# Unscaled softmax rows, 1/sum through DRAM, and masks by GpSimd in an attention and feed-forward kernel

## The chip, the cores and the metric

One core of one Trainium2 chip. Its engines are TensorE (PE in the profile; its weight loads are PEld), VectorE (DVE), ScalarE (ACT), GpSimd (POOL) and SyncE (SP, which here issues nearly all DMAs). The metric is device time in microseconds for one execution.

## The reference

Batch 8, 8 heads, 576 rows, head size 64; then a feed-forward block on 4608 rows of 512 with a hidden size of 768.

```python
scores = q @ k.T / sqrt(64)                    # for each batch and head
thresh = max(scores, -1) - tau                 # tau = 0.02
scores = where(scores >= thresh, scores, -1e9)
attn = exp(scores - max(scores, -1))
attn = attn / (sum(attn, -1) + 1e-9)
x = (attn @ v), heads side by side             # 4608 x 512
h = maximum(maximum(x @ w1, x @ w2), x @ w3)
out = h @ w_out
```

So each row of the softmax keeps only the scores within tau of its maximum, and each row is divided by its own sum.

## The kernel before

**Tiles.** Four heads of one batch make a quad (16 quads, `g`). Its 4 x 576 rows are 18 half tiles of 128 rows by 576 scores: nine chunks `c` of two halves `r` (the two pairs of heads). In all there are 144 chunks, 288 halves. Chunk 4 of a quad holds the ninth 64 rows of two heads together, so that its partitions 0 to 63 and 64 to 127 belong to different heads. Two quads make a batch's 512 columns of x, on which the feed-forward block runs: six hidden tiles of 128 for each of three weights (`hid` in `ffn`), then the output chunks (`outp`, and `ninth` for the odd 64 rows). The last batch is cut into two parts of rows (`SPLIT`).

**The path of a half.** `scores` puts 128 x 576 into PSUM (TensorE). `maximum` (DVE) copies it to a tile `z` in SBUF, negated, and takes the row's maximum in the same instruction (`accum_out`). Then one of four ways, set by a digit for each half in `MASKED`:

- 0: `threshold` (DVE, one column), Prelu (ACT) that flattens all above the threshold's distance, Exp with the row sum (ACT). Two passes on ACT.
- 1: Exp (ACT), then a compare-and-multiply with the row sum (DVE, `scalar_tensor_tensor`). One pass on each.
- 2 and 3: as 0 and 1, with ACT reading the scores from PSUM (`direct`) and not from `z`.

All of these write into `z` in float32. When both halves of a chunk have their sums (`sm`, two columns), `reciprocals` takes 1/sum (DVE), and `normalized` multiplies each half by it on GpSimd, into the bf16 tile `P` of 128 x 1152. `turned` issues a DMA transpose of `P` from SP into `ptq`; with it `product` multiplies by v into PSUM as x transposed (64 columns of x by 576 rows, two heads on 128 partitions). x is evacuated to `xt` in bf16, one half of the products by DVE (`on_vector`), the other by ACT (`on_scalar`).

**Buffers.** `z` has 9 tiles, and from the 72nd half on two more are borrowed from the pool `stage`, whose other use is loading the weights in the first part (`half_of_z`). `P` has 6 tiles. PSUM is four slots of 128 x 1024, shared by everything that TensorE writes.

**The order.** `_Ordered` ties the instructions of each engine to the order in which the program names them. That order is written out by hand as a text, `ORDER`: each letter issues one step (with a digit for the PSUM slot where it starts one), and `issue` gives the letters their meaning. S: scores of a half; m: `maximum`; s: `threshold`; e: `exponents`; n: the second ACT pass; k: the DVE mask; r: `reciprocals`; p: a scaling pass on GpSimd; t: `turned`; T: transposes of q and k, evacuated by a (ACT) and c (DVE), with copies q on GpSimd; O: a product, evacuated by x (ACT) or w (DVE); F and B: the two halves of a feed-forward group, evacuated by h (ACT), v (DVE) and u (ACT); l: loads; o and i: stores; g and z: loading and casting of the weights; y: casts of v. So an engine does the steps that fall to it in the order of the letters, and waits where one is not ready. The line number of nearly all instructions in the profile is that of the helper in `_Ordered` (L93).

Of the kernel before, what the change touches and what calls it, by code (L numbers as in the profile page):

```python
# [15 lines left out]
OP = AluOpType  # L16
# [5 lines left out]
FLAT = 2.0 ** -100  # L22

MASKED = """
232222322322222222021032222202332122123122200200111000000000100000000011
000010111020011000101000000001100001001000010011111100000000100100000000
110010030111000100010000000001010100001110001011010100110000000000000000
100101101011000000120000001010000000110011100000001110001000010011111021
# [6 lines left out]
MORE_Z = 72  # L35
# [5 lines left out]
llllllglllT0laclT1laclzllqqS0qqS1meS2mS3lmlT0enlkS1ylmlT2eamelrnpS3leqlmnyS1qcapS0emtnrcS3pmnT2qmepgrelS1qya  # L41
gS0pmelT2mqnS3tcpemqS2nlkT1eytaS0rmnT1kpermS3yS2enczrmS1qT0enmepnqtS3nprmaymgpeS0lptS2mppT0mtpS1enencnqsS3re
rmtpS0mS1penmS3lqnsS2mtperpekzllmT0tmpenkT1pgS3eearnS0petmnqrS2meqlnpS3lmnplsS2cetpremS1pS0nmplermtzeS3mnS2p
mtnpmS3rkpS1leektS0emnrpmemptS1eekS2pO3mktS0rennmpermT2pnS1wptemS3prkyO0tmeakS2pgS1enxlnrmS0lpesS2mezT3mS1np
mgntspcS2eqrseT3mtpeS0srmapS1mnT2ptS3mnqO0ceqmeO1prswnptnkS3pxS0meF1meS2zBresmT0qghF3klpF2nkBtaS1sveS0pemF3B
nyrrsmyBepT1svS0hpcT2nS3zmaS1erpgsF2mntpsBmnS3yvF1etssT0myeBprS2cnpS3mnS0ympelF2epF3lmBnzslssvS0htBrqmeS2vpn
S1gF0sepmF3teqBmF2erssvpBtnBkphF0eS1vtS3znmF2nrBmqteS1rpvBnS3pmlnF0pmgeS1qsBsrhmS3pevS2npS1mF0npsO3ermpesmO2
zewepgsskBxtT3nF1vS2nklBarS0mlphS3mtepF2sS1rmnyBmetF3pvT0eBpcnS2tzT1nvS0asmzS3temS2qeS1meF0trkpmS3lenpBmnlys
reklpF1umerpskS3upBeoketmS0uS2umpS3tesmS1qeT0myO2nqlrsnlprcO3etqsmepwS0xptS1mnF3psnmS2BlerskpS1thF0meF3pmeBF
2ktnBveBsrS1nvpS0hmyF3emF2npBrssT0eprtvBaF1kS3nqvBeF0myhyS2kyleF3mBelBvnpS2snsS0vptemS1pnF3rmpT2tnBmpeF0scS1  # L50
htBrnmpF3erT2rpvlBasS1pstvnS2pmeF0pS3emtBqnmT2S1hcqS3empF2eS0rsqmtS1epsmBeF3pmnF0stsvBeBknF2klhF1BvelS0nrvpB
emT3pS2arvS0ptnS3mpnO1smtesrkpeF2swnlrpmeT0S1qtescS3epBmnpmnT0trskS3paS1umS0ulqmeS3lmyS1nopS2smelS0rmeS3psmn
O1ypersmqO2etkpemO0lewqxlknpS3tS1keF2momS3lexF0ktT1enkBercpnsBpumN1ertkphkF3jS0rursS1empBnmF2ptS0vpS1smeF3yt
BsnsmBpnvS0pT1hmF2atT3srepS0cF1eprBsmeqF3vnByBynvplS2nsS0plmhS1mteS2mF0nF3mteS1rrspBnmS2pelvBlepF1smT0leqBvl
aS2rkhF3oqnsS0mtS1epmBeqsF2ssmtS0epvBeyF1mnF3vpBesrS0ktphBermS1npT2svO0nytmpncT3eS1wF2nrmS0aBrsmnqF3vnT1pS0c
eBptsF2mhpS1eS3pmteS0qmBeO1spmnkteF3rvnpT0BsskapS2xvS0erS1qmtnS3pmnF2mqlespmeS1rtkBepresmT3puS1cuS0ptmnS3pS2
meyS1lrekpF0tnsmempO3lekteskO2nrsmpeBkpxrnwS1uptS3muS2pnmF0yoeS1mF3lesymBtnS2srkpS1hmBeF0spveF2ertBmpT3nrsvS
1paBlmpnS0tS3qhmF1epsmS2leBymF3tevF0nBknlS1rsvpS2esmqnBF3srmhpS1epS0tmeF2pssBrempBtesvS0ynF1mT3lnpBvF0lhsrcS
2tnT1mBnF3valS2nrBsqmeF0pvS1epS2meBptsmS3eqF1hmT2peBcS3tnskT2O0arkplnmO2lerpvewptS3xkpS1nF2meF0sstreBsmpS3nv
pBnmS1tS2hmT3eF0rmpnF1cBpnBrevptT3S2apvS0qmtS3S1enmqF2esrsqmiepmleS0soykeS1plBnmemtS3ukS0uT1snrlO2cpekynO1me  # L60
ymeF3pwxskteS0keS1BrrnkopmF2pmS0BqeuurtsmF1phS3srnpS2meT0ptBmeS3ykpaN2esvempF0tS1jkpF3ermBeS2ptvnS1pmBnS0rls
hsmpS2elF3mqntS1mpF0nsrBskpeF2lsmBetBpveF1yhvS3lnkS2lesF0mytnBmBerqsS3veF2lpvnF1pBsmT0htBceF3rT2vnpBsaS0pvnF
1qmtS2nBsrnmT0pS3hrcpF2esS1mpteS0rmpS3emBpntF1svqnS0ssBmpeoT2vO3lamtneF1wS0nrlBpmeS3qsrS2hsmS0pnmF1eptS3smeB
pmF2ntS0veS3rsmnpS1BnpO0veytrempS2empS3xsmS1tekF0nsknlT2rmpBelmlpnscS3quS1umyS2eorT0kpeO3tmeyO1ewlepsmF3etka
rknS2qklT0nBmxespcS2eryF0mpF1uskpuBtnS2BhmqF3nsvS0peS2srmtpF1eBmpeF0srvnBptS2hyS3pmeF1lmeBlBevtF3nkT2S0arrvp
BnS2mphS1smpF0ntS3smnpBmeF1lsT2esvlF3nrBrcptBnvpS2eS0qmlhS1tsnprsmT3F2epmS0aptBemF3yevS1oS0nqmBnpsrS2mnF1ptv
S0epmBeS3mthS2skeF0F1snmlBeklO3ersvpnrmByepF0swT2eqtBvnqF3ssrcS1hpiBmpT0S2vaptS1snmS0pnT3mqF2tecT1BarmS3pnS1
vqeS0mF2pesrmnptmS3npT1seS0qctBeymqermpS1eS3mpuF0nmtuskS1eS2klnS3smBesrsepO1upmemO2txrkpukeO3wnkpS0xS2emF3et
rmS1pnBssspmF2hS0rtepS3mnBpmF1etS0veF3mnN2rnpBpjF0evtF2esBkBkhF1nsvS3eBmBevO3hrkS2pwnS1mnF3prmS2eptsF0mnBpsS
1sevyS2terBmpeF3svS1iyepBmoS0yhmtF2ekF3nBsmS1ersBvpnF0pmeF2BvteS1hBmF3rsS0vpeF1rknpBBmnO2vhptO0xrpnS3pwS2trm  # L70
npS0mnF3pmteF1pBeBvtS0rS2vpS3empF1ktkF0kBereskpemBkperumO2uptO3xpN1wtenkO2jrF3pxF1hpF2nvF3tvF1rhF2pvF3pvF1hF
2tvF3vF1hF2voF3vF1ohF2vF3vF1hF2vO3vO1wF2xuuF1oF0hiF3vF1vF0hF3vF1vF0hF3vF1vF0hF3vF1vF0hF3vF1vF0huF3vF1ovF3uoF
0uoN1fjdi
# [31 lines left out]
def kernel(  # L105
# [44 lines left out]
    def weight_loads():  # L150


        def piece(dst, src):
            my = {}

            def load():
                my["t"] = stage.tile([128, 4 * 256], F32, name="stage")
# [19 lines left out]
    small = ctx.enter_context(tc.tile_pool(name="small", bufs=6))  # L177
# [177 lines left out]
    halves_of_z = iter(range(1 << 20))  # L355

    def half_of_z():

        n = next(halves_of_z)
        if n >= MORE_Z and (n - MORE_Z) % (ZBUFS + 2) >= ZBUFS:  # L360
            return stage.tile([128, 4 * 256], F32, name="stage")[:, :S]
        return zz.tile([128, S], F32, name="z")

    def maximum(c, r):

        z = c["z", r] = half_of_z()
# [8 lines left out]
    def threshold(c, r):  # L375
        th = c["th", r] = small.tile([128, 1], F32, name="th", bufs=5)
        vector.tensor_scalar(out=th, in0=c["nm", r], scalar1=-1.0, scalar2=tau, op0=OP.mult, op1=OP.subtract)
# [22 lines left out]
    def normalized(c):  # L400
        c["P"] = P = pp.tile([128, W], BF16, name="P")
        for n in range(2):
            pool.tensor_scalar(out=P[:, n * S:(n + 1) * S], in0=c["z", n],
                                    scalar1=c["rs"][:, n:n + 1], scalar2=1.0, op0=OP.mult, op1=OP.mult)
            if n:
                line["t"].append(c)
            yield
# [7 lines left out]
    def product(L, r, target, part=None):  # L415
# [26 lines left out]
        def on_vector():  # L442
            ps = st["ps"]
            dst = target(L["b"])[:, 2 * L["qd"] + r, :]
            vector.tensor_copy(out=dst[:, lo:hi], in_=ps[:, base:base + hi - lo])

        def on_scalar():
            ps = st["ps"]
            dst = target(L["b"])[:, 2 * L["qd"] + r, :]
            scalar.activation(out=dst[:, lo:hi], in_=ps[:, base:base + hi - lo], func=AF.Copy)  # L450
        p = _Piece((L["b"], L["qd"], r, part), first)
        p.vector = on_vector if r == 0 else None
        p.scalar = on_scalar if r == 1 else None
# [25 lines left out]
    def ffn(b, part):  # L479
# [87 lines left out]
        def ninths_of_two():  # L567
# [11 lines left out]
            def done():  # L579
                ob = hp_.tile([128, DM], F32, name="ob9", bufs=1)  # L580
# [12 lines left out]
        def ninth():  # L593
# [10 lines left out]
            def done():  # L604
                ob = hp_.tile([128, DM], F32, name="ob9", bufs=1)[:, 0:DM // 2]
# [36 lines left out]
    Ls, xts, stores, stores9, ends, ninths = {}, {}, [], [], [], []  # L642
# [20 lines left out]
    vector.memset(vrs[2], 0.0)  # L663
    for t in vrs[0:2]:
# [33 lines left out]

    def flow(what, fn):
        while True:  # L700
            yield from fn(line[what].pop(0))
# [5 lines left out]
                O=products(), F=pieces(), N=iter(lambda: ninths.pop(0), None))  # L707
    line = {k: [] for k in "menkrptahvuxwcqsjf"}
    casts = iter([w[1] for w in wl])
    loads = iter([w[0] for w in wl])  # L710
    flows = dict(p=flow("p", normalized), q=flow("q", lambda x: swapped(*x)),
# [7 lines left out]
    def issue(what, where):  # L719
# [10 lines left out]
        elif what == "O":  # L730
            p = next(todo["O"])
            p.first(where)
            for k, fn in (("x", p.scalar), ("w", p.vector)):
                if fn:
                    line[k].append(fn)
# [11 lines left out]
        elif what == "m":  # L747
            c, r = line["m"].pop(0)
            maximum(c, r)
            line["e"].append((c, r))  # L750
            if not masked(c["g"], c["idx"], r) and not direct(c, r):
                line["s"].append((c, r))
        elif what == "s":
            threshold(*line["s"].pop(0))
# [4 lines left out]
        elif what in "nk":  # L759
            c, r = line[what].pop(0)  # L760
# [69 lines left out]
```

## Time and profile before

| | |
|---|---|
| time of three runs | 446.69, 446.92 and 449.09 us; median 446.92 |
| profiled execution | span of 444.8 us from its first to its last instruction; a time of its own beside that is not listed, and the median of the runs lies 2.1 us above the span |
| busy | PE 422.4, DVE 392.8, ACT 403.0, POOL 311.9 us |
| mean granted TensorE clock | 0.988 |
| DMA | 88.5 MB, 213,959 packets |

The page gives the busy time of an engine as the union of its instructions, and a string of 40 digits, tenths of busy time in 40 equal slices of the span. In a group's row stand the engine, the operation, out<-in with the names of the tiles, the shapes, the count, then busy us, mean ns of one, and the idle time before them with what ended it. `z<-sc` is written from the scores in PSUM; `stage` in place of `z` is a borrowed buffer.

### The profile page before, as it was taken

The numbers are of one execution on the slowest core, as the hardware profiler recorded it, in microseconds if no ns is written. First come the engines' busy times: TensorE is split into PE (matmuls) and PEld (weight loads), VectorE is DVE, ScalarE is ACT, GpSimd is POOL, SyncE is SP. The second block draws the span as 40 slices with busy tenths as digits, with TensorE's granted clock in tenths as the row PEclk, the third lists the DMA queues.
The fourth block names the chain that finished last, engine by engine and source line by source line (L and its number), as shares of the span: only waits on it lengthen the run. The fifth ranks groups of instructions, "written<-read, shape, count | busy, mean of one in ns | idle before, by whom it ended". The sixth has DMA issues, their size and how long they took to land.

```text
span 444.8 us, 14254 instructions
## 1 busy us (share of the span) xinstructions
PE 422.4 (95%) x5188; PEld 320.2 (72%) x5190; DVE 392.8 (88%) x1228; ACT 403.0 (91%) x836; POOL 311.9 (70%) x420
## 2 busy tenths in 40 slices
PE   7767789999999999999999999999999999999996
PEld 6334347787788767787788777788688886787873
DVE  3887999999999999999999999998999998899642
ACT  3999999999999999999999999899999999987632
POOL 2799989997878687696785877676676685457400
PEclk8998999999999999999999999999999999999999
DMA  7999999999999999699899999989999977487633
GB/s 188 275 293 199 291 169 269 235 243 262 229 180 194 212 222 292 125 256 167 143 234 189 230 198 203 209 168 210 208 206 194 244 151 105 83 179 136 145 116 108
DMA packets 213959, 88.50 MB, mean 199 GB/s; under 512 B 189184, under 2 KB 202240, under 8 KB 213888
## 3 DMA queue, kind: packets, MB, share of 16 engines
q1 hardware_dynamic: 213360, 86.96, 95.9%
q8 instruction: 41, 0.67, 0.6%
q10 hardware_dynamic: 528, 0.62, 0.5%
q14 instruction: 30, 0.25, 0.2%
HBM read 35.65 MB, written 9.44 MB: 101 GB/s over the span
## 4 chain that ended last, share of the span: by engine, by line
PE 86%; ACT 5%; DVE 4%; issue 2%; DMA 1%; SPq 0%; DVEq 0%; ACTq 0%
PE ph L93 32%; PE sc L93 32%; PE po L93 10%; PE o L93 9%; ACT z L93 5%; PE tp L93 3%; DVE z L93 3%; DMA qm<-in_q_dram 1%; ACT qt L93 1%; SPq L93 0%; DVE xt L93 0%; DVE hm L93 0%; DVE stage L93 0%; DVE rs L93 0%; ACT ob L93 0%
## 5 line engine op out<-in xcount | busy, mean ns | idle before, releaser
L93 POOL TENSOR_SCALAR P<-z,rs 128x576 bf16<-128x576 f32 x250 | 200.6, 814 | 63.3 <-DVE rs L93 28.1
L93 DVE TENSOR_SCALAR_CACHE_REDUCE z<-sc 128x576 f32<-128x576 f32 x250 | 183.7, 750 | 14.8 <-PE sc L93 10.1
L93 PE MATMUL sc<-kt,qs 64*128 64x256 f32 (+2 forms) x640 | 182.6, 423 | 5.7 <-DVE z L93 2.3
L93 PE MATMUL sc<-kt,qt 64*128 64x320 f32 (+2 forms) x640 | 182.4, 433 | 5.2 <-ACT z L93 3.3
L93 PE MATMUL ph<-xt,w 64*128 64x288 bf16 (+2 forms) x2160 | 170.8, 283 | 0.1
L93 PEld LDWEIGHTS <-w 64*128 64x128 bf16 (+1 forms) x2160 | 130.1, 94 | 28.6 <-issue 4.3
L93 ACT ACTIVATE z<-z 128x576 f32<-128x576 f32 x174 | 117.6, 679 | 0.1
L93 PEld LDWEIGHTS sc<-kt,qs 64*128 64x128 f32 (+1 forms) x640 | 92.4, 180 | 25.7 <-DVE z L93 5.7
L93 ACT ACTIVATE z<-z,th 128x576 f32<-128x576 f32 x143 | 106.2, 769 | 5.0 <-DVE th L93 4.2
L93 PEld LDWEIGHTS sc<-kt,qt 64*128 64x128 f32 (+1 forms) x640 | 91.9, 179 | 19.7 <-ACT z L93 5.9
L93 DVE SCALAR_TENSOR_TENSOR z<-z 128x576 f32<-128x576 f32 x76 | 62.2, 830 | 0.5 <-ACT z L93 0.5
L93 PE MATMUL po<-wo,hT 64*128 64x512 bf16 (+3 forms) x454 | 53.5, 354 | 0.3
L93 POOL COPY qs<-qt 64x640 f32<-64x640 f32 (+3 forms) x66 | 43.0, 652 | 10.8 <-ACT qt L93 7.2
L93 ACT ACTIVATE z<-z,nm 128x576 f32<-128x576 f32 x68 | 50.6, 767 | 0.0
L93 DVE TENSOR_TENSOR hm<-ph,hm 128x576 bf16<-128x576 f32 (+2 forms) x54 | 37.0, 686 | 9.2 <-PE ph L93 8.9
L93 ACT ACTIVATE hm<-ph 128x576 bf16<-128x576 f32 (+2 forms) x54 | 31.8, 589 | 13.4 <-PE ph L93 12.8
L93 POOL TENSOR_SCALAR P<-stage,rs 128x576 bf16<-128x576 f32 x38 | 30.4, 804 | 19.3 <-ACT z L93 5.4
L93 PEld LDWEIGHTS <-hT 64*128 64x128 bf16 (+2 forms) x456 | 30.0, 95 | 16.5 <-issue 2.3
L93 DVE TENSOR_TENSOR hT<-ph,hm 128x576 bf16<-128x576 f32 (+2 forms) x54 | 37.0, 686 | 4.0 <-PE ph L93 2.3
L93 PE MATMUL o<-ptq,vb 128*64 128x64 bf16 (+2 forms) x544 | 39.0, 281 | 0.0
L93 ACT ACTIVATION_READ_ACCUMULATOR z<-z 128x1 f32 x174 | 34.3, 197 | 0.0
L93 PEld LDWEIGHTS <-vb 128*64 128x64 bf16 x544 | 23.3, 111 | 12.8 <-issue 4.9
(45 smaller groups left out, 431.6 us busy)
## 6 DMA issues: line engine op xcount, KB each, us to landing
vm<-in_v_dram SPq DMA_DIRECT2D x32, 256.0 KB, 4.8
qm<-in_q_dram SPq DMA_DIRECT2D x15, 512.0 KB, 5.0
km<-in_k_dram SPq DMA_DIRECT2D x15, 512.0 KB, 5.3
out_dram<-ob SPq DMA_DIRECT2D x14, 512.0 KB, 4.0
stage<-in_moe_w_dram SPq DMA_DIRECT2D x9, 512.0 KB, 5.2
ptq<-P SPq DMA_TRANSPOSE x144, 4.0
vr<-in_v_dram SPq DMA_DIRECT2D x16, 128.0 KB, 3.4
stage<-in_moe_w_out_dram SPq DMA_DIRECT2D x3, 512.0 KB, 4.9
```

Of the source, the lines that this page charges most:

```text
L93: ins = fn(*a, **kw)
```

## The change

- `P` is written directly by the last step of a half, in bf16 and unscaled (ACT's Exp or DVE's mask). `normalized`, its letter p and the scaling pass are gone.
- The sums of a quad (or of a quad's part, in the last batch; 18 units) stand in one tile `sm` of 20 columns. `reciprocals` works once for a unit: one reciprocal of the columns and one that moves the odd 64 rows to the partitions of their own place (three in the last batch's second part, one in its first), then a 32 x 32 block transpose of 128 x 32 on DVE. The letter D stores the result to a tile `rows` in DRAM (32 x 128), and R loads it back twice, broadcast over 64 partitions each, into a tile of `stage`, 128 x 2 x 576.
- All evacuations of x are on DVE now, as a product of PSUM and that tile (letter w); x of the letters is gone.
- A fifth digit, 4, stands at 13 halves, ten of them among the first 72: `threshold` takes the negated maximum plus tau, `set_apart` (letter b) makes three passes on GpSimd: subtract the threshold and multiply by 2 to the 100th (into `P`, bf16), maximum with 0, add to `z`. Then one Exp with the row sum on ACT (letter X). The digits 2 become fewer, 1 more.
- `z` borrows no buffers of `stage`; the two tiles of `stage` are 1152 wide; `ob9` uses a `z`. `small` has 8 buffers.
- `ORDER` and `MASKED` are new as a whole.

```diff
+FAR = 2.0 ** 100
...
-        if n >= MORE_Z and (n - MORE_Z) % (ZBUFS + 2) >= ZBUFS:
-            return stage.tile([128, 4 * 256], F32, name="stage")[:, :S]
-        return zz.tile([128, S], F32, name="z")
+    def by_pool(c, r):
+        return by_mask[2 * number[c["g"], c["idx"]] + r] == "4"
...
+        if by_pool(c, r):
+            vector.tensor_scalar(out=th, in0=c["nm", r], scalar1=tau, scalar2=None, op0=OP.add)
...
+    def half_of_p(c, r):
+        if "P" not in c:
+            c["P"] = pp.tile([128, W], BF16, name="P")
+        return c["P"][:, r * S:(r + 1) * S]
...
+    def set_apart(c, r):
+        z, m = c["z", r], half_of_p(c, r)
+        pool.tensor_scalar(out=m, in0=z, scalar1=c["th", r], scalar2=FAR, op0=OP.subtract, op1=OP.mult)
+        pool.tensor_scalar(out=m, in0=m, scalar1=0.0, scalar2=None, op0=OP.max)
+        pool.tensor_tensor(out=z, in0=z, in1=m, op=OP.add)
...
     def numerators(c, r):
-        z, acc = c["z", r], c["sm"][:, r:r + 1]
-        if masked(c["g"], c["idx"], r):
-            vector.scalar_tensor_tensor(out=z, in0=z, scalar=thr, in1=z,
+        z, p, acc = c["z", r], half_of_p(c, r), sum_of(c, r)
+        if by_pool(c, r):
+            scalar.activation(out=p, in_=z, func=AF.Exp, bias=c["nm", r], scale=-1.0, accum_out=acc)
+        elif masked(c["g"], c["idx"], r):
+            vector.scalar_tensor_tensor(out=p, in0=z, scalar=thr, in1=z,
                                         op0=OP.is_ge, op1=OP.mult, accum_out=acc)
         else:
-            scalar.activation(out=z, in_=z, func=AF.Exp, scale=-1.0 / FLAT, accum_out=acc)
-    def reciprocals(c):
-        c["rs"] = small.tile([128, 2], F32, name="rs")
-        vector.reciprocal(c["rs"], c["sm"])
-    def normalized(c):
-        c["P"] = P = pp.tile([128, W], BF16, name="P")
-        for n in range(2):
-            pool.tensor_scalar(out=P[:, n * S:(n + 1) * S], in0=c["z", n],
-                                    scalar1=c["rs"][:, n:n + 1], scalar2=1.0, op0=OP.mult, op1=OP.mult)
...
+            scalar.activation(out=p, in_=z, func=AF.Exp, scale=-1.0 / FLAT, accum_out=acc)
...
+    def reciprocals(g, part, n):
+        L, t = Ls[g], turns[n % 2]
...
+            vector.reciprocal(new[:, :, f:f + 9], sums[:, :, f:f + 9])
...
+            vector.reciprocal(new[to, :, at:at + 1], sums[of, :, was:was + 1])
+        vector.transpose(t[:, 1, :], t[:, 0, :])
...
+    def scale_rows(g, part):
+        s["rows"] = rows.tile([32, 128], F32, name="rows")
+        sync.dma_start(out=s["rows"].rearrange("j (b t) -> b j t", b=4), in_=s["t"][:, 1, :])
+    def scale_tile(g, part):
+        s["R"] = stage.tile([128, W], F32, name="stage").rearrange("p (r n) -> p r n", r=2)[:, :, 0:n]
+        src = s["rows"].rearrange("j t -> (j t)")[0:2560].rearrange("(r i y) -> i r y", i=2, y=640)
+        for i in range(2):
+            sync.dma_start(out=s["R"][64 * i:64 * i + 64],
+                           in_=src[i, :, o:o + n].unsqueeze(0).to_broadcast([64, 2, n]))
...
-        def on_vector():
-            vector.tensor_copy(out=dst[:, lo:hi], in_=ps[:, base:base + hi - lo])
-        def on_scalar():
-            scalar.activation(out=dst[:, lo:hi], in_=ps[:, base:base + hi - lo], func=AF.Copy)
+        def done():
+            vector.tensor_tensor(out=dst[:, lo:hi], in0=ps[:, base:base + hi - lo],
+                                 in1=scales[2 * L["b"] + L["qd"], part]["R"][:, r, :], op=OP.mult)
```

More of the change, by code (lines that the diff above doesn't have):

```diff
@@ L74 @@
+wwF3F2uhvF1F3vF2hvF0vF3hF1vF2vF0hF3F2F0vhF1ovvF3F0hoF1vF2vivF3N0F2uojiuoF3fd
 """
@@ L156, in load @@
             def load():
-                my["t"] = stage.tile([128, 4 * 256], F32, name="stage")
+                my["t"] = stage.tile([128, W], F32, name="stage")[:, :1024]
                 sync.dma_start(out=my["t"].rearrange("p (k f) -> p k f", k=src.shape[1]), in_=src)
@@ L176 @@
     pt_pool = ctx.enter_context(tc.tile_pool(name="pt", bufs=2))
-    small = ctx.enter_context(tc.tile_pool(name="small", bufs=6))
+    small = ctx.enter_context(tc.tile_pool(name="small", bufs=8))
+    rows = ctx.enter_context(tc.tile_pool(name="rows", bufs=2, space=bass.MemoryType.DRAM))
     xp = ctx.enter_context(tc.tile_pool(name="xp", bufs=2))
@@ new lines, in numerators @@
+        c["halves"] = c.get("halves", 0) + 1
+        if c["halves"] == 2:
+            line["t"].append(c)
+    turns = [one.tile([128, 2, 32], F32, name=f"turn{x}") for x in range(2)]
+    def reciprocals(g, part, n):
+        L, t = Ls[g], turns[n % 2]
+        f = ninth_first(L["b"])
+        two = lambda a: a.rearrange("p (r x) -> p r x", x=10)
+        new, sums = two(t[:, 0, 0:20]), two(L["sm"])
+        if part is None:
+            vector.reciprocal(new[:, :, f:f + 9], sums[:, :, f:f + 9])
+        else:
+            five = lambda a: a.rearrange("p (h x) -> p h x", x=5)
+            c0, c1 = part[0], min(part[-1], 3) + 1
+            vector.reciprocal(five(t[:, 0, 0:20])[:, :, c0:c1], five(L["sm"])[:, :, c0:c1])
+        if part is None or 4 in part:
+            if part is not None:
+                vector.reciprocal(new[:, :, 4:5], sums[:, :, 4:5])
+            to, of = (slice(64, 128), slice(0, 64)) if f else (slice(0, 64), slice(64, 128))
+            at, was = (0, 5) if f else (9, 4)
+            vector.reciprocal(new[to, :, at:at + 1], sums[of, :, was:was + 1])
+        vector.transpose(t[:, 1, :], t[:, 0, :])
+        scales[g, part] = dict(t=t)
@@ L641 @@
     number = {x: n for n, x in enumerate(steps)}
-    Ls, xts, stores, stores9, ends, ninths = {}, {}, [], [], [], []
+    Ls, xts, stores, stores9, ends, ninths, scales = {}, {}, [], [], [], [], {}
     def x_of(b):
@@ L663 @@
     vector.memset(vrs[2], 0.0)
+    for t in turns:
+        vector.memset(t[:, 0], 1.0)
     for t in vrs[0:2]:
@@ L697, in products, with units @@
                         yield product(Ls[g], r, x_of, part)
+    def units():
+        n = 0
+        for b in range(B):
+            for part in parts_of(b):
+                for g in (2 * b, 2 * b + 1):
+                    yield g, part, n
+                    n += 1
     def flow(what, fn):
@@ L732, in issue @@
             p.first(where)
-            for k, fn in (("x", p.scalar), ("w", p.vector)):
-                if fn:
-                    line[k].append(fn)
+            line["w"].append(p.evac)
         elif what in "FN":
@@ L749, in issue @@
             maximum(c, r)
-            line["e"].append((c, r))
+            if not by_pool(c, r):
+                line["e"].append((c, r))
             if not masked(c["g"], c["idx"], r) and not direct(c, r):
@@ L753, in issue @@
         elif what == "s":
-            threshold(*line["s"].pop(0))
+            c, r = line["s"].pop(0)
+            threshold(c, r)
+            if by_pool(c, r):
+                line["b"].append((c, r))
+        elif what == "b":
+            c, r = line["b"].pop(0)
+            set_apart(c, r)
+            line["X"].append((c, r))
         elif what == "e":
@@ L758, in issue @@
             line["k" if masked(c["g"], c["idx"], r) else "n"].append((c, r))
-        elif what in "nk":
-            c, r = line[what].pop(0)
-            if "sm" not in c:
-                c["sm"] = small.tile([128, 2], F32, name="sm")
-            else:
-                c["summed"] = True
-            numerators(c, r)
-        elif what == "r":
-            c = made[line["r"].append(0) or len(line["r"]) - 1]
-            assert c["summed"]
-            reciprocals(c)
-            line["p"].append(c)
+        elif what in "nkX":
+            numerators(*line[what].pop(0))
+        elif what == "r":
+            g, part, n = next(todo["r"])
+            reciprocals(g, part, n)
+            line["D"].append((g, part))
+        elif what == "D":
+            g, part = line["D"].pop(0)
+            scale_rows(g, part)
+            line["R"].append((g, part))
+        elif what == "R":
+            scale_tile(*line["R"].pop(0))
         elif what == "t":
```

112 lines of the change are left out of this document (55 added, 57 removed).

## The prediction

> **What bounds the kernel now.** I read the page first, then the busy time by stretches, then the engines' instructions in order of time. On the page:
>
> ```profile
> span 444.8 us, 14254 instructions
> PE 422.4 (95%) x5188; PEld 320.2 (72%) x5190; DVE 392.8 (88%) x1228; ACT 403.0 (91%) x836; POOL 311.9 (70%) x420
> ...
> PE   7767789999999999999999999999999999999996
> ...
> ACT  3999999999999999999999999899999999987632
> ...
> PE 86%; ACT 5%; DVE 4%; issue 2%; DMA 1%; SPq 0%; DVEq 0%; ACTq 0%
> ```
>
> PE looks like the bound: busy for 95% of the span, and 86% of the chain that ended last. Two rows speak against it, one of the chain in order of time and one of the groups by form:
>
> ```profile
> 329.87 1.96 PE ph L93 x32
> ```
>
> ```profile
> L93 PE MATMUL ph<-xt,w 64*128 64x288 bf16 x2016 | 152.8, 283 | 0.1
> ```
>
> Unhindered, 32 of these matmuls take 1.96 us, 61 ns each, so these 2016 need 123 us; they are shown busy for more than that, because a pipelined matmul that waits inside its line counts as busy. PE therefore has slack that the 95% hides. The stretches, cut where 72 of the 288 row maxima are through (the row of the groups up to 98.4) and where all are (412.6):
>
> ```profile
> L93 DVE TENSOR_SCALAR_CACHE_REDUCE z<-sc 128x576 f32<-128x576 f32 x72 | 52.7, 751 | 7.0 <-PE sc L93 5.3 <-POOL P L93 1.2
> ```
>
> ```profile
> core 0: us, PE busy (x) PEld busy (x) DVE busy (x) ACT busy (x) POOL busy (x), PEclk, DMA share, GB/s
> 0.00:10.00 10.00, 7.21 (x66) 6.16 (x68) 2.48 (x11) 2.71 (x5) 1.54 (x7) 0.88 0.70 180
> 10.00:98.40 88.40, 74.42 (x784) 48.85 (x783) 80.40 (x250) 86.66 (x187) 79.46 (x107) 0.96 1.13 246
> 98.40:412.60 314.20, 313.00 (x4069) 244.41 (x4067) 296.45 (x940) 301.81 (x619) 226.69 (x303) 1.00 0.99 193
> 412.60:444.80 32.20, 27.78 (x280) 20.78 (x278) 13.51 (x33) 11.83 (x28) 4.17 (x6) 0.99 0.44 128
> ```
>
> From 10 to 98.4 ACT is busy for 86.7 of 88.4 us (98%), DVE 80.4, and PE stands idle for 14. From 98.4 to 412.6 ACT has 301.8 of 314.2 (96%), DVE 296.5 (94%). The last 32 us are PE work behind the last scores. So ACT sets the pace, DVE close behind it; each works in a fixed order, and the few idle per cent are the two and PE waiting for one another. What one half tile costs there is the distance between starts, not the duration, since neighbours overlap:
>
> ```profile
> 216.23 0.69 ACT L93 ACTIVATE z<-z 128x576 f32<-128x576 f32 x1
> 216.80 0.20 ACT L93 ACTIVATION_READ_ACCUMULATOR z<-z 128x1 f32 x1
> 216.90 0.77 ACT L93 ACTIVATE z<-z,th 128x576 f32<-128x576 f32 x1
> 217.56 0.77 ACT L93 ACTIVATE z<-z,nm 128x576 f32<-128x576 f32 x1
> 218.23 0.68 ACT L93 ACTIVATE z<-z 128x576 f32<-128x576 f32 x1
> ```
>
> ```profile
> 217.00 0.75 DVE L93 TENSOR_SCALAR_CACHE_REDUCE z<-sc 128x576 f32<-128x576 f32 x1
> ...
> 217.68 0.16 DVE L93 RECIPROCAL rs<-sm 128x2 f32<-128x2 f32 x1
> 217.76 0.74 DVE L93 SCALAR_TENSOR_TENSOR z<-z 128x576 f32<-128x576 f32 x1
> ...
> 218.42 0.15 DVE L93 TENSOR_SCALAR th<-nm 128x1 f32<-128x1 f32 x1
> 218.49 0.75 DVE L93 TENSOR_SCALAR_CACHE_REDUCE z<-sc 128x576 f32<-128x576 f32 x1
> ```
>
> On ACT: Exp with its accumulator 0.67 (216.23 to 216.90; the read is the last 0.10), Prelu 0.66, one-pass Exp 0.67. On DVE: maximum 0.68, reciprocal 0.08, masking multiply 0.66, threshold 0.07.
>
> **The change, part by part.** The rows that price the rest, groups by form:
>
> ```profile
> L93 POOL TENSOR_SCALAR P<-z,rs 128x576 bf16<-128x576 f32 x250 | 200.6, 814 | 63.3 <-DVE rs L93 28.1 <-ACT z L93 11.6 <-DVE th L93 7.4
> L93 DVE SCALAR_TENSOR_TENSOR z<-z 128x576 f32<-128x576 f32 x76 | 62.2, 830 | 0.5 <-ACT z L93 0.5
> L93 DVE TENSOR_TENSOR hm<-ph,hm 128x576 bf16<-128x576 f32 x42 | 31.5, 751 | 0.8 <-PE ph L93 0.6
> L93 ACT ACTIVATE z<-sc,nm 128x576 f32<-128x576 f32 x39 | 28.3, 746 | 2.9 <-DVE z L93 2.9
> L93 DVE CAST xt<-o 128x576 bf16<-128x576 f32 x14 | 10.5, 749 | 0.5 <-PE o L93 0.5
> L93 ACT ACTIVATE xt<-o 128x576 bf16<-128x576 f32 x14 | 9.0, 640 | 0.2
> L93 POOL CAST vb<-vm 128x1024 bf16<-128x1024 f32 x16 | 18.1, 1130 | 3.9 <-DMA vm<-in_v_dram 3.2 <-PE sc L93 0.6
> L93 DVE RECIPROCAL rs<-sm 128x2 f32<-128x2 f32 x144 | 22.0, 157 | 2.0 <-ACT z L93 1.4 <-ACT stage L93 0.2
> ```
>
> *ACT.* Counting MASKED: digits 0, 1, 2, 3 stand at 169, 78, 33, 8 before and at 169, 87, 12, 7 after, with 13 fours. Two-pass halves (0 and 2) fall by 21, all of them read from PSUM: 0.746 less the 0.10 overlap is 0.64, plus 0.67, so 21 x 1.31 = -27.5. One-pass halves (1 and 3) grow by 8: +5.4. A four is one Exp with an accumulator, 0.67 + 0.10: 13 x 0.77 = +10.0. ACT loses its 18 evacuations of x: 14 x 0.54 and four short ones, -8.8. Net -20.9: ACT 403.0 -> 382.1.
>
> *DVE.* Eight more masking multiplies, +5.3; 13 more thresholds, +0.9; 144 reciprocals go, -11.5. The 18 evacuations come from ACT as a product of PSUM and SBUF. The TENSOR_TENSOR row has that shape at 751, the present cast 749, so the multiplication is free and the move costs 14 x 0.67 and four short ones, +10.9. New are 36 reciprocals and 18 transposes, of no known row: between 0.08 (the present one's distance) and 0.16 (its duration) each, 4 to 9; I take the middle, +6.5. The masking multiply averages 830 ns but 740 at 217.76: the rest is contention for SBUF with GpSimd's scaling passes, which average 814 and take 740 where they meet none:
>
> ```profile
> 218.00 1.11 POOL L93 TENSOR_SCALAR P<-stage,rs 128x576 bf16<-128x576 f32 x1 [0.36 <-POOL vr L93]
> 219.09 0.74 POOL L93 TENSOR_SCALAR P<-z,rs 128x576 bf16<-128x576 f32 x1
> ```
>
> The first of these overlaps that multiply, the second overlaps none. With the 288 scaling passes gone, 86 x 0.09, less a little for the new passes: -7. Net +5.1: DVE 392.8 -> 397.9.
>
> *GpSimd.* 231 us of scaling go. Each four adds three passes, written in place: two of one input (0.74 to 0.81, as the scaling) and a two-input add, which no row shows. The cast vb reads 1024 elements in 1.13; the add reads 1152, so 1.3, in all 2.8 a half, bounds 2.2 (three at 0.74) and 4. Ten of the 13 fall within the first 72 halves, 28 us there, while the scaling frees more than 50: GpSimd's 79.5 in that stretch becomes about 55, and the 28 hide behind ACT and DVE, unless one is late (third rival). The Trainium skill, GPSIMD Engine Reference, Engine selection, tells one to put elementwise work on VectorE, GpSimd being about twice slower with two inputs; its 2.6 cycles an element at 1.2 GHz give 1.25 us for the add, as an estimate. By that advice the 13 would be masking multiplies, 13 x 0.66 = 8.6 us more on DVE and 1.3 less on ACT; no run here shows the add yet.
>
> *The path from a half to its product.* Today P waits for the second half's sum, the reciprocal and the scaling pass, and SP's queue for P (its waits; then its instructions in order of time):
>
> ```profile
> SPq L93 <- POOL P L93: 130.9, 83, 6.0
> ```
>
> ```profile
> 217.86 0.58 SPq L93 DMA_DIRECT2D k<-in_k_dram  x1
> 218.53 1.39 SPq L93 DMA_TRANSPOSE ptq<-P  x1
> ```
>
> After it a transpose can start when both halves have their numerators. That frees z buffers sooner; the two stage buffers that z borrowed are given up for it. SP's queue gains 18 stores and 36 loads at about 0.6 of issue, 32 us; with 144 transposes at 1.39 and about 140 other DMAs at 0.6 (the letters l, g, o, i of ORDER) it held 284 us and now holds 316 of 445: room, but each D and R stands behind transposes, and an R that waits for its D holds the transposes behind it.
>
> *Where it lands.* To 98.4 us: by the digits there (25, 10, 30, 7 before; 32, 12, 12, 6 and ten fours after) ACT changes by +9.3 - 23.6 + 0.7 + 7.7 - 1.1 = -7.0, DVE by about -1. The larger load falls from 86.7 to 79.7, the mean of the two from 83.5 to 79.6. If the larger sets the time, 7 us go; if their mean does, 4; I take 5. From there to 412.6: ACT -13.9 to 287.9, DVE +6 to 302.5. The larger load rises by 0.7, the mean falls by 4.0. Now the second engine has slack and GpSimd no part in the chain, so I take -2.5, nearer the mean. The end is PE's and stays; I add +0.7 for late scales (first rival). Sum -6.8: span 438.0. The median of the runs (446.92) is 2.1 above this span, which holds for a median of 440.
>
> **The rivals.** *The scale comes late (slower).* Before a unit's first evacuation (a head quad of one batch, 18 units) lie reciprocals and transpose, a store to DRAM, its landing, two loads, theirs:
>
> ```profile
> vm<-in_v_dram SPq DMA_DIRECT2D x32, 256.0 KB, 4.8
> km<-in_k_dram SPq DMA_DIRECT2D x1, 256.0 KB, 5.5
> out_dram<-ob SPq DMA_DIRECT2D x3, 64.0 KB, 2.6
> ```
>
> About 0.4 + 2.6 + 0.6 + 4.8 = 8.4 us (the loads are 295 KB each), 9.1 with km's 5.5, 10 if each stands behind half a transpose. Against this I set the DVE work that ORDER puts between r and the unit's first w, from the distances above: 6.5, 7.8, 8.0, 8.0, 8.9, 9.1, 9.4, 9.5, 9.5 in nine units, 10.7 to 15.6 in the others; divided by DVE's 94%. At 8.4 us about 1.7 is missing over all units, most of it at the last but one, where PE's tail hides a part; at 10 it is 9; at 12 it is 28. DVE stands still then, with every maximum behind it, and PSUM fills. It decides from about 9.7; without the 0.7 the sum is 439.4, so at 10 us 448, at 11, with 18 missing, 457. For it: the loads read one row 64 times over, share the DMA engines with the transposes, and need a stage buffer that the unit two before must have left. Against: loads of their size land in 4.8 to 5.5. By the Trainium skill, DMA: Bandwidth & Descriptors, Anatomy of one DMA (about 2.0 us and bytes at 436 GB/s, given for GpSimd's queue) the chain would be some 6 us, as an estimate, and nothing missing; vm's 4.8 for 256 KB disagrees.
>
> *PE is the bound after all.* If the waits hidden in PE's lines belong to PE, nothing moves but idle time at the start: 446 to 447. For it the 86% of the chain, against it the 61 ns.
>
> *GpSimd's fours are late.* At 4 us a half, with ACT's Exp queued behind, 10 x 1.2 in series gives the front's 5 back: 445.
>
> *The larger gain.* If the front gives 7 and the stretch after it 4 to 5: 434 to 436.
>
> **How the numbers follow.** The runs shown spread by 0.5%, about what a measurement can tell from no change: 444.7 to 449.2 is "same". Forecast (436 to 444) 0.50, larger gain 0.10, PE bound 0.10, late fours 0.06, late scale 0.24, of which half lies below 453. Faster 0.60, same 0.16, slower 0.24. The range, 431 to 453, leaves out the far half of the late scales and a little below; the forecast's own is 436 to 444.
>
> **What would show it.** Right: ACT near 382 and DVE near 398 busy; the 72nd maximum at about 93 instead of 98.4; the masking multiply near 750 ns; GpSimd near 120. Wrong: rows of DVE xt waiting for a DMA into stage, more than 5 us in all (late scale); ACT's Exp of a four waiting for POOL z (late fours); ACT and DVE falling as said with the stretch from 98.4 unchanged (PE bound); a TENSOR_TENSOR into xt well over 751 (the product is not free).

## The result and the profile after

The kernel after takes 502.43 us (median; 498.59 to 504.37), the kernel before, beside it, 447.05: a ratio of 1.123 [1.117, 1.128]. The forecast was 440.0 with a range of 431 to 453 and 0.6 for faster, so it was wrong in sign and by 62 us. The profiled execution took 501.1 us with a span of 499.2.

From the page of the kernel after:

```profile
span 499.2 us, 13800 instructions
...
PE 440.2 (88%) x5188; PEld 325.4 (65%) x5190; DVE 407.5 (82%) x1187; ACT 386.4 (77%) x789; POOL 153.8 (31%) x171
...
ACT  4765865994798988388966899887998997998621
POOL 3999999510510142068210113010102201010000
PEclk9887697997799999899998999999999999999999
...
PE 40%; DMA 15%; DVE 13%; issue 6%; ACT 5%; SPq 3%; POOL 1%; DVEq 0%; ACTq 0%; POOLq 0%
```

ACT fell about as forecast (403.0 to 386.4; 382 was said), and 55 us were lost all the same. So it wasn't lost to work but to standing still: ACT is busy for 77% of a longer span, with holes in its string, and DMA, 1% of the chain before, is now 15%. The string of POOL is full just where the ten early fours stand. The mean TensorE clock fell from 0.988 to 0.952; as half-speed time, (1 - 0.952) x 499.2 / 0.5, that is 48 us against 11.

The stretches of the kernel after, cut again at the 72nd and the last row maximum:

```profile
core 0: us, PE busy (x) PEld busy (x) DVE busy (x) ACT busy (x) POOL busy (x), PEclk, DMA share, GB/s
...
10.00:112.80 102.80, 80.39 (x768) 56.02 (x766) 82.25 (x241) 77.19 (x164) 81.33 (x71) 0.87 0.98 214
112.80:467.00 354.20, 324.15 (x4070) 242.25 (x4067) 305.76 (x894) 295.47 (x598) 70.62 (x92) 0.97 1.00 199
467.00:499.20 32.20, 27.77 (x278) 20.54 (x276) 15.10 (x36) 9.75 (x22) 0.00 (x0) 0.99 0.49 127
```

14 us are lost in the first (88.4 before), 40 in the second (314.2), none at the end. The waits of the kernel after (total, times, longest) name two causes that the kernel before doesn't have:

```profile
ACT P L89 <- POOL z L89: 23.2, 10, 4.9
DVE xt L89 <- DMA stage<-rows: 22.6, 7, 7.8
...
DVE z L89 <- DMA out_dram<-z: 4.2, 2, 2.7
```

The first is the Exp of a four, which waits for GpSimd. The second is x, which waits for its scale: the row that the prediction named as the sign of the late scale. The third, DVE waiting for a store out of a `z` tile, it had not named. Its groups on GpSimd, for the first:

```profile
L89 POOL TENSOR_SCALAR P<-z,th 128x576 bf16<-128x576 f32 x13 | 29.6, 2278 | 3.7 <-DVE th L89 2.4 <-issue 0.2
L89 POOL TENSOR_SCALAR P<-P 128x576 bf16<-128x576 bf16 x13 | 21.5, 1653 | 1.1
...
L89 POOL TENSOR_TENSOR z<-z,P 128x576 f32<-128x576 f32 x13 | 16.8, 1291 | 1.1
```

Three passes take 2.28 + 1.65 + 1.29 = 5.2 us and not 2.8. For the second, the third unit's scale; first SP's queue, then DVE, in order of time:

```profile
103.23 6.97 SPq L89 DMA_TRANSPOSE ptq<-P  x3
110.25 0.64 SPq L89 DMA_DIRECT2D vm<-in_v_dram  x1
110.99 0.59 SPq L89 DMA_DIRECT2D rows<-turn  x1
...
113.52 1.64 SPq L89 DMA_DIRECT2D qm<-in_q_dram  x1
115.27 1.23 SPq L89 DMA_DIRECT2D stage<-rows  x2
```

```profile
116.65 0.08 DVE L89 DVE_READ_ACCUMULATOR z<-sc 128x1 f32 x1
124.53 0.76 DVE L89 TENSOR_TENSOR xt<-o,stage 128x576 bf16<-128x576 f32 x1 [7.80 <-DMA stage<-rows]
```

DVE's transpose of the sums had ended at 107.05. D went out at 110.99, behind SP's transposes; R at 115.27, behind a 512 KB load of q; and R's data took 8 us from the end of its issue. That makes 17.5 us, with DVE still for the last 7.8. In the seven units where DVE waited for it, this path took 7.3 to 17.6 us, 12.3 in the mean: 5.7 until R went out and 6.6 from there to the first use. TensorE stops as well, and its clock with it, in stretches cut there:

```profile
117.50:119.70 2.20, 0.03 (x3) 0.00 (x0) 0.00 (x0) 0.24 (x2) 1.04 (x1) 1.00 1.11 233
119.70:124.50 4.80, 0.00 (x0) 0.00 (x0) 0.00 (x0) 0.00 (x0) 0.00 (x0) 0.50 1.34 209
124.50:129.90 5.40, 4.55 (x31) 3.74 (x33) 3.62 (x9) 2.69 (x5) 1.94 (x3) 0.50 0.88 243
129.90:132.00 2.10, 2.10 (x33) 1.85 (x31) 1.91 (x6) 1.32 (x4) 1.57 (x2) 0.98 0.87 253
```

So a standstill is paid for twice: TensorE has no matmul from 117.53 to 125.35, 7.8 us, and then goes on at half its clock until 129.97, another 4.6. The Trainium skill, TensorE: Matmul & The Clock Gate, What's actually happening, tells of two states only, half and full, set by windows of about 3.4 us that run on their own. The trace agrees in the two values and in the length of the half clock, 10.2 us or three windows; that the half comes after an idle window it doesn't bear out exactly, since the clock fell 2.2 us after the last matmul.

### The profile page after: what moved, and what is told of

It reads as the page before. It is cut to its first block, busy times and chain, and to the rows that moved or that the text cites. A ratio compares the mean times of both kernels' runs of the same rounds, so it can differ in the third digit from the quotient of the medians.

```text
span 499.2 us, 13800 instructions
## 1 busy us (share of the span) xinstructions
PE 440.2 (88%) x5188; PEld 325.4 (65%) x5190; DVE 407.5 (82%) x1187; ACT 386.4 (77%) x789; POOL 153.8 (31%) x171
## 4 chain that ended last, share of the span: by engine, by line
PE 40%; DMA 15%; DVE 13%; issue 6%; ACT 5%; SPq 3%; POOL 1%; DVEq 0%; ACTq 0%; POOLq 0%
PE ph L89 18%; PE sc L89 12%; DMA stage<-rows 7%; DVE z L89 6%; PE po L89 6%; SPq L89 3%; PE o L89 3%; ACT z L89 3%; DMA ptq<-P 3%; DMA rows<-turn 2%; DVE P L89 2%; ACT P L89 2%; DVE hm L89 2%; PE tp L89 2%; DMA out_dram<-z 2%
## 5 line engine op out<-in xcount | busy, mean ns | idle before, releaser
L89 DVE TENSOR_SCALAR_CACHE_REDUCE z<-sc 128x576 f32<-128x576 f32 x288 | 209.3, 751 | 31.4 <-PE sc L89 19.0
L89 ACT ACTIVATE z<-z,th 128x576 f32<-128x576 f32 x169 | 125.6, 766 | 8.5 <-DVE th L89 8.3
L89 ACT ACTIVATE P<-z 128x576 bf16<-128x576 f32 x181 | 121.6, 674 | 1.4 <-DMA ptq<-P 1.1
L89 PEld LDWEIGHTS sc<-kt,qs 64*128 64x128 f32 (+1 forms) x640 | 97.5, 186 | 36.7 <-DVE z L89 10.3
L89 PEld LDWEIGHTS sc<-kt,qt 64*128 64x128 f32 (+1 forms) x640 | 97.0, 186 | 33.2 <-DVE z L89 7.9
L89 DVE SCALAR_TENSOR_TENSOR P<-z 128x576 bf16<-128x576 f32 x94 | 77.0, 824 | 0.7 <-DMA ptq<-P 0.4
L89 ACT ACTIVATE z<-z,nm 128x576 f32<-128x576 f32 x87 | 64.9, 765 | 0.0
L89 POOL CAST vb<-vm 128x1024 bf16<-128x1024 f32 x16 | 17.0, 1061 | 97.6 <-PE sc L89 46.1
L89 DVE TENSOR_TENSOR xt<-o,stage 128x576 bf16<-128x576 f32 (+2 forms) x36 | 24.3, 683 | 24.8 <-DMA stage<-rows 22.6
L89 ACT ACTIVATE ob<-po 128x512 f32<-128x512 f32 x31 | 17.1, 592 | 25.0 <-PE po L89 17.1
```

What stands on the lines that cost most here:

```text
L89: ins = fn(*a, **kw)
```

## The experiments

Theory A: GpSimd's passes are the loss (late fours). Theory B: the scale's path is (late scale). Theory C: the new order itself, or the buffers, cost time.

### The fours on ACT instead of GpSimd (e1_prelu)

```diff
     def set_apart(c, r):
-        pool.tensor_scalar(out=m, in0=z, scalar1=c["th", r], scalar2=FAR, op0=OP.subtract, op1=OP.mult)
-        pool.tensor_scalar(out=m, in0=m, scalar1=0.0, scalar2=None, op0=OP.max)
-        pool.tensor_tensor(out=z, in0=z, in1=m, op=OP.add)
+        exponents(c, r)
```

> The 13 fours are done by ACT's Prelu and Exp (as a 0) at the same places of the order; GpSimd makes no masking pass, all else is the changed kernel (502.4). Theory A, the three GpSimd passes (2.22 + 1.65 + 1.28 us, some 5.4 with gaps, where 2.8 was forecast) fill GpSimd for the first 83 us and hold ACT and DVE: the 72nd maximum comes at 95 to 100 instead of 112.8, quad 7's stretch loses another 8 us, time 475 to 482. Theory B, the late scale is the main loss: the 72nd maximum moves by less than 5 us, time 490 to 500. Theory C, the new order itself is at fault: time above 495.

481.39 us, ratio 1.076 [1.072, 1.080]: 21 us come back, although ACT now does the 13 extra passes (busy for 393.1 us, 386.4 in the kernel after). The 72nd maximum ends at 102.2 us instead of 112.8, which is half of the 21 and 2 us later than Theory A had it; the rest comes after it. The scale's wait is still there:

```profile
DVE xt L89 <- DMA stage<-rows: 17.9, 10, 6.8
```

### A scale that is ready (e2_ready_scale) and both (e3_both)

```diff
     def scale_rows(g, part):
-        s["rows"] = rows.tile([32, 128], F32, name="rows")
-        sync.dma_start(...)
+        pass
     def scale_tile(g, part):
-        s["R"] = ...
+        pass
...
-                                 in1=scales[...]["R"][:, r, :], op=OP.mult)
+                                 in1=ready[:, 0:(hi - lo) // 2]..., op=OP.mult)
```

> No store to DRAM and no load back: x's evacuation multiplies by a constant tile that is always there, so x is not divided by its sums; reciprocals and transposes stay, the fours stay on GpSimd. Theory A: 490 to 500 (only the 22.6 us of DVE's waits for the scale at most, much of it taken up again behind GpSimd). Theory B: these 22.6 us go, and with them the half-speed clock of PE after each standstill, time 465 to 475. Theory C: above 490.

> Both edits: no GpSimd masks and a scale that is always there (x is not divided by its sums). Theories A and B together: nothing of the 55 us is left and the sum of the prediction without late scales should hold, 435 to 447. Theory C: above 455, with DVE and ACT waiting for PE or one another where neither GpSimd nor a load is late.

The ready scale gives 471.74, ratio 1.054 [1.051, 1.057]: 31 us come back, more than the 22.6 that DVE waits in the profile. e2 takes away the 18 stores and 36 loads themselves and not only their lateness; how the rest of the 31 divides between TensorE's clock behind each wait and what these DMAs cost the others wasn't separated. Both edits give 457.9 (455.6 to 460.2), ratio 1.023 [1.011, 1.036]. So on top of the other, the scale is worth 23 (e1 to e3) and the fours 14 (e2 to e3), and each of them 7 more by itself. Up to the 72nd maximum it is mostly the fours: it ends at 112.8 us after, 114.5 in e2, 102.2 in e1, 96.8 in e3. From there on it is mostly the scale: 386 us to the end of the span after, 356 in e2, 376 in e1, 357 in e3. A and B both hold. But e3 isn't back at 447, as A and B together had it (435 to 447); what is left is C's part. In its profile DVE waits for a store once, and for P tiles that their transposes still read:

```profile
DVE P L89 <- DMA ptq<-P: 4.1, 2, 2.3
ACT P L89 <- DMA ptq<-P: 4.0, 3, 1.9
DVE z L89 <- DMA out_dram<-z: 3.6, 1, 3.6
```

### The odd rows' output out of a stage buffer (e6_ob9_apart)

On top of e3:

```diff
-                ob = zz.tile([128, S], F32, name="z")[:, 0:DM]
+                ob = stage.tile([128, 1024], F32, name="stage")[:, 0:DM]
```

> As e3_both (457.9; no GpSimd masks, scale always there, x not divided by its sums), but the buffer of the odd 64 output rows is a tile of the pool stage instead of one of the nine z tiles. If DVE's 3.6 us standstill at 184.6, on the store of that buffer, and what PE's clock loses after it are a real loss: 451 to 455. If the time is taken up again elsewhere: 457 to 458.

451.99, ratio 1.011 [1.007, 1.015]: 6 us more between the medians, though e3's two runs lie 4.6 apart. The first such output is written at 175 us, so up to there e3 and e6 do the same; from the 96th maximum to the last, where they differ, the profiles have 288.2 and 284.1 us, 4.1 less. So the buffer is worth 4 to 6. A `z` tile that is also an output tile is held until its store has landed, and the next maximum that gets this tile waits, with all of DVE's queue behind it. Of 55 us 5 are left.

### Why GpSimd's passes took 5.2 us (e4_pool_ops, e7_add_multiply)

e4_pool_ops runs forms of the passes on GpSimd alone, six of each, and computes nothing of the reference:

> GpSimd alone, six times each on 128 x 576 with no other engine at work: the scaling pass (multiply, multiply, f32 to bf16), subtract and multiply, add and multiply, multiply and add, subtract alone, subtract and multiply to f32, subtract and maximum, maximum bf16 to bf16, maximum f32, multiply bf16, and the two-input add with bf16 and with f32. It computes none of the reference. If the durations belong to the operations: 0.74 for multiply-multiply, 2.2 for subtract-multiply, 1.65 for the maximum in bf16, 1.27 for the add. If they come from contention in the kernel: 0.74 to 0.85 for all with one input, 1.0 to 1.3 for the add.

```profile
L42 POOL TENSOR_SCALAR submul<-zin,th 128x576 bf16<-128x576 f32 x6 | 13.3, 2211 | 0.5
L45 POOL TENSOR_SCALAR subonly<-zin,th 128x576 bf16<-128x576 f32 x6 | 10.3, 1725 | 0.5
...
L47 POOL TENSOR_SCALAR maxbf<-binn 128x576 bf16<-128x576 bf16 x6 | 9.9, 1645 | 0.1
L50 POOL TENSOR_TENSOR addfb<-zin,binn 128x576 f32<-128x576 f32 x6 | 7.6, 1272 | 0.0
...
L41 POOL TENSOR_SCALAR mulmul<-zin,th 128x576 bf16<-128x576 f32 x6 | 4.5, 744 | 0.5
L43 POOL TENSOR_SCALAR addmul<-zin,th 128x576 bf16<-128x576 f32 x6 | 4.5, 744 | 0.5
```

The durations are those of the kernel, with nothing beside them: they belong to the form of the pass, not to contention. Subtract-and-multiply takes three times as long as add-and-multiply on the same tiles. e7 uses that on top of e2 (the threshold is negated, DVE does it in the same instruction):

```diff
-scalar1=c["th", r], scalar2=FAR, op0=OP.subtract, op1=OP.mult)
+scalar1=c["th", r], scalar2=FAR, op0=OP.add, op1=OP.mult)
```

> As e2_ready_scale (471.7; scale always there, x not divided by its sums, fours on GpSimd), but the first GpSimd pass adds the negated threshold and multiplies (0.744 us alone) instead of subtracting and multiplying (2.211). Theory A, GpSimd is the bound of the first 86 us: ten halves times 1.48 in series, the 72nd maximum 9 to 14 us earlier than 114.5 and some 3 us more at quad 7: 456 to 463. If GpSimd's length is not what counts but only that Exp waits in ACT's order: above 466.

459.66, ratio 1.028 [1.023, 1.034]: 12 us come back through one pass that is 1.5 us shorter. The 72nd maximum ends at 101.9 us (114.5 in e2), and ACT's wait falls from 20.9 to 12.2, first e2's row, then e7's:

```profile
ACT P L89 <- POOL z L89: 20.9, 9, 4.9
```

```profile
ACT P L89 <- POOL z L89: 12.2, 6, 4.7
```

### Where the scale's path is slow (e5_gpsimd_queue, e10_scale_trip_alone)

e5 is e1 with D and R issued by GpSimd, so that neither stands behind SP's transposes and loads:

```diff
-        sync.dma_start(out=s["rows"]...
+        pool.dma_start(out=s["rows"]...
-            sync.dma_start(out=s["R"][64 * i:64 * i + 64],
+            pool.dma_start(out=s["R"][64 * i:64 * i + 64],
```

> As e1_prelu (481.4), but the store of the sums' reciprocals and the two loads of the scale are issued by GpSimd, which has little else to do, at the same places of the order. If the scale is late because it stands in SP's queue and behind the loads that SP issued ahead of it, transpose to evacuation shrinks from up to 16 us to 8 to 10 and DVE's 17.9 us of waits for the scale mostly go: 463 to 472. If the landing itself is slow whatever the queue: 478 to 484. If GpSimd, waiting in order for the store to land, holds the copies of q behind it: above 484.

502.48, ratio 1.124 [1.116, 1.133]: 21 us worse than e1, in the range of the third case. Its waits, and the landing of R's full-size loads:

```profile
POOL rows L89 <- DVE turn L89: 93.2, 13, 16.3
DVE xt L89 <- DMA stage<-rows: 34.9, 8, 12.5
POOL stage L89 <- DMA rows<-turn: 32.9, 15, 4.6
```

```profile
stage<-rows POOLq DMA_DIRECT2D x28, 288.0 KB, 6.2
```

The same trouble on another queue: GpSimd stands for 93.2 us at a D that waits for DVE and for 32.9 at an R that waits for D, with its q copies and casts behind them. What the third case named isn't what the time went to, though: no engine waits more than 0.5 us for GpSimd's copies or casts in this trace, while DVE's wait for the scale grows from 17.9 to 34.9. In the eight units where DVE waits, R goes out 5.4 us in the mean after the transpose of the sums, about as late as from SP (5.7), and is used 8.7 later (6.6 from SP): issued first at 108.29 in one unit and there at 118.68, at 386.28 and 397.84 in another. So GpSimd's queue is no cure, and e5 doesn't show what a free queue would give.

e10 does the trip by itself, eight times in a row (store, wait, two loads, a DVE copy), and none of the reference:

> The scale's trip by itself, eight times one after the other with no other DMA in flight: the store of 128 x 32 to DRAM, the two broadcast loads of 64 x 2 x 576, a DVE copy that waits for them. It computes none of the reference. If the trip is slow in itself (a store to DRAM, one row read 64 times): 3.5 to 5 us from the store's issue to its landing and 6 to 9 for the loads, 10 to 14 a round. If it is slow only among the transposes and the 512 KB loads: 2 to 2.6 and 3 to 5, a round of 6 to 8.

```profile
DVE acc L40 <- DMA stage<-rows: 60.5, 8, 8.3
```

```profile
stage<-rows SPq DMA_DIRECT2D x16, 288.0 KB, 4.6
```

It wasn't alone: in the first six rounds SP issued three output stores of 256 KB behind D and three behind R, and the DMA engines were busy for more than 80% of most of these rounds. Even so a trip takes 60.5 / 8 = 7.6 us in the mean and R lands in 4.6 (median); the six rounds with stores took 7.3 to 8.3, the last two, without any, 7.0. So the prediction's chain without its DVE part, 2.6 + 0.6 + 4.8 = 8.0, is right for a trip that no queue holds up, and such stores beside it cost it about 1 us. In the kernel the mean of the seven was 12.3. Up to R's issue it was 5.7 there and 2.2 in the six rounds, from there to the use 6.6 and 5.6: of the 4.5 us more, 3.5 lie before R goes out, 1 behind it. In the unit above these are the 3.9 us before D, and 3.7 between D's issue and R's, of which D's landing explains about 1.4 (in the units with a free queue R goes out 2.0 to 2.1 us after D's start, D's issue of 0.6 among them). How the landing alone, without the queue, fares among the transposes wasn't tested.

### P unscaled in the kernel before, and its tiles (e9, e11)

e9 is the kernel before with the scaling pass left out (its x is not divided by the sum), P written by the last step of a half, and nothing else changed. e11_five_p and e11_seven_p change the number of P tiles; the last has 8 `z` tiles for it.

```diff
-        c["P"] = P = pp.tile([128, W], BF16, name="P")
         for n in range(2):
-            pool.tensor_scalar(out=P[:, n * S:(n + 1) * S], ...)
```

> The kernel before with one part of the change alone: P written directly and unscaled, GpSimd's 288 scaling passes gone, and nothing in their place (x is not divided by its sums); order, masks and reciprocals as before (447.0). The prediction's step: ACT and DVE set the pace, the contention costs DVE 7 us, P is ready earlier: 442 to 445. Rival: the scaling pass was hidden and the engines wait for one another as before: 446 to 447.5. Rival: P's six tiles are held longer, from the first numerator until the transpose has read them, so that ACT and DVE wait for a free P: above 448.

> As e9_before_unscaled with five tiles of P, all else the same (x not divided by its sums). If P tiles are short: the waits of ACT and DVE for the transposes grow to 20 us or more and the time to above 455. If they are hidden: 450 to 452.

> As e9_before_unscaled (450.6; unscaled P in the order before, x not divided by its sums) with seven tiles of P and eight of z in place of six and nine. If ACT's and DVE's 11 us of waits for a P tile that its transpose has not read yet are what made it slower than 446.7: 445 to 448. If not, or if z is now short: 450 or more.

With 5, 6 and 7 tiles 464.05, 450.64 and 445.95 us, ratios 1.038 [1.033, 1.043], 1.007 [1.004, 1.009], 0.997 [0.995, 0.999]. (With 6 the ten runs go from 447.6 to 453.2, and the profile is of the slowest.) ACT's wait, in that order, each row from its own run; DVE adds 1.2, 2.5 and nothing:

```profile
ACT P L93 <- DMA ptq<-P: 17.1, 8, 3.7
```

```profile
ACT P L93 <- DMA ptq<-P: 8.7, 8, 2.7
```

```profile
ACT P L93 <- DMA ptq<-P: 1.6, 2, 1.1
```

To leave out 288 GpSimd passes for nothing in return makes the kernel slower by 0.7%; only with a seventh tile it gains 1 us. The scaling was hidden, and its P tile had been cheap: it was held from the scaling to the transpose, now from the first numerator of a chunk, which includes the second half's masking.

### Less work for TensorE (e12_bf16_scores)

The kernel before with q and k in bf16 for the scores, which rounds them:

```diff
-            L[n + "t"] = qk.tile([128, 2, S], F32, name=n + "t")
+            L[n + "t"] = qk.tile([128, 2, S], BF16, name=n + "t")
-                L["qs"] = qk.tile([128, 2, S], F32, name="qs")
+                L["qs"] = qk.tile([128, 2, S], BF16, name="qs")
```

> The kernel before with q and k transposed into bf16 tiles, so that the scores' matmuls are bf16 and take a fraction of PE's time (the scores are rounded); ACT, DVE and the order are the same. If PE sets the pace after the first 98 us (it is busy there for 313 of 314 us, and stretches of 24 halves last the same in kernels with other masks and orders): that stretch falls from 314 until ACT is full, 302 to 306, and the time to 430 to 438. If ACT and DVE set it, as the prediction had it: 445 to 447.

441.91, ratio 0.988 [0.986, 0.989], between what the two views expected. From the 96th to the last maximum, in e12, in the kernel before, and in e6 (where the change's ACT and DVE loads meet neither scale nor fours):

```profile
132.10:407.80 275.70, 234.27 (x3236) 160.26 (x3234) 264.07 (x842) 267.33 (x554) 200.57 (x270) 0.99 0.98 192
```

```profile
131.30:412.60 281.30, 280.10 (x3658) 217.97 (x3654) 265.07 (x840) 269.12 (x553) 200.21 (x270) 1.00 0.97 189
```

```profile
133.80:418.00 284.20, 281.90 (x3648) 210.19 (x3644) 271.50 (x798) 262.63 (x533) 45.51 (x71) 1.00 0.94 188
```

Taking 45.8 us from TensorE shortens the stretch by 5.6, and ACT is then busy for 97% of it. So TensorE has a part in the time there, and it is a small one. In e6 ACT has 6.5 us less and DVE as much more, and the stretch is 2.9 longer; but e6 differs from the kernel before in its order, its `P` and its `z` tiles too. That all three engines stand so near the time that relieving one shows the next fits these rows, but isn't shown for ACT and DVE apart.

## Why the prediction was wrong

**The forecast's work.** Most of it came: ACT 386.4 (382.1 forecast), and the 28 full-size products into `xt` take 750 ns as forecast, so the multiplication is free. DVE came to 407.5 and not 397.9, mainly because the masking multiply did not get faster: 94 at 824 ns instead of 750 are 7 us.

```profile
L89 DVE SCALAR_TENSOR_TENSOR P<-z 128x576 bf16<-128x576 f32 x94 | 77.0, 824 | 0.7 <-DMA ptq<-P 0.4
```

The 26 of them that overlap work on GpSimd take 1.01 us in the mean (0.75 to 1.83), the other 68 take 0.75, so work on GpSimd does lengthen it, as the prediction said. But it laid all of it to the scaling passes: without these and without the fours the mean is still 783 ns (e1), and in the kernel before without its scaling passes 790 (e9). About half of the relief came, and the longer passes of the fours took it back. GpSimd came to 153.8 instead of about 120, mostly 13 times 2.4 more.

**First failed step: the fours at 2.8 us.** The passes were priced by the scaling row (0.74 to 0.81, a multiply-multiply) because they have its shape and input count. The bound from above, 4, was too low as well: 5.2. In the front that is ten times 2.4 us more, 52 us of passes in place of 28, beside GpSimd's casts and copies: 81 us of work in one in-order queue, in a stretch that was to last about 83. "Hidden" was then false, and ACT's Exp waited for ten of the thirteen. The rival was there with its mechanism, at 0.06 and 445 us, where it only gave back the gain: its own 10 x 1.2 is 12 us, which would have been 452, and with 5.2 the same formula gives ten times 2.4, 24 us lost. The fours were worth 14 to 21.

**Second failed step: the chain of 8.4 us.** It was added from transfers of the kernel before and is right where no queue holds it up (e10). In the kernel, without the DVE part, it was 12.3 in the mean of the seven units where DVE waited, and 3.5 of the 4.5 us over e10 arose before R went out, where D and R stand in SP's queue. The prediction did list what would lengthen it (each D and R standing behind transposes, shared DMA engines) and then put +0.7 into the sum. By its own line 12 us would leave 28 missing, and e2 gives 31: the rival's mechanism was right, its input was chosen too low, and the range ended at 453. That 28 and 31 lie so close is luck in part: the 28 count 12 us for all 18 units, while DVE waited in seven, for 22.6.

**Third failed step: P's path as pure gain.** That this frees `z` buffers sooner no run prices; P's own tiles were not counted, and they are held longer (e9 against e11). Nor was the `z` that now serves as `ob9`, 4 to 6 us (e6).

**Fourth failed step: ACT sets the pace, TensorE has slack.** The time of the matmuls was read rightly, the conclusion was too strong: e12 gains 5.6 us in that stretch with TensorE relieved. From the 72nd maximum on, the forecast was -2.5 because the mean of ACT and DVE falls. In e6 the time from the 96th on follows the larger load, which rises by 2.4, or TensorE, which rises by 1.8; the two aren't told apart. Of the front's 5 us, with fours and scale both gone, 1.6 to 4.0 came: the 72nd maximum is at 96.8 in e3 and at 94.4 in e6 (93 forecast, 98.4 before), two executions of the same work up to there. Both give it back right after: 36.0 and 39.3 us for the next 24 halves against 32.8. In e6 the rows of waits there show TensorE waiting 2.3 us for a q load and ACT and DVE 2.4 for P tiles. What the rest is stays open.

**The sum.** From the kernel after: fours 21 (e1), scale 23 more (e3), the store out of `z` 6 by the medians (e6), 5 left, which no run divides: the order, the P tiles, the shift of load to DVE, and the passes that e1, e3 and e6 put back on ACT. The late scale and the late fours came together, each larger than its rival; the prediction had them exclude each other.

## What to carry to other kernels

Price an operation by a row of the same operation, not only of the same shape: two operations on the same tiles differed here by a factor of three, and an in-order engine that such a factor would fill decides the sign. A trip through DRAM in front of a shared in-order engine must be priced with what stands ahead of it in the queue, where most of the difference arose here, and it can cost more than the wait that is shown: behind the wait of 7.8 us TensorE went on at half its clock for 4.6. Work that is hidden costs nothing to keep: before it is removed, ask which buffer it kept short-lived.

## What the runs showed of the hardware

- GpSimd on 128 x 576 elements: add-multiply, multiply-add and multiply-multiply by two scalars 0.74 us, but subtract-multiply 2.21, subtract 1.73, maximum 1.65 to 1.70, and a single multiply from bf16 to bf16 1.65; the two-input add 1.14 (float32) and 1.27 (with one bf16). The prediction's estimate for that add from the Trainium skill, 1.25, lies between the two. The Trainium skill's word that GpSimd's one-input work runs at about line rate (GPSIMD Engine Reference, Engine selection) does not hold for the subtracts and the maxima, two to three times slower than the 0.74.
- A standstill of TensorE of 7.8 us brought half its clock for 10.2 us, 4.6 of them after its work had begun again.
- A store of 16 KB to DRAM and its reload over 128 partitions take 7.0 us from SBUF to SBUF with no other transfer beside them, 7.3 to 8.3 with six output stores of 256 KB a round, and 7.3 to 17.6 in this kernel, where they stood in SP's queue.
